# Value products moved into the next pair's first slot in a fused attention and feed-forward kernel, with V casts and part of the K/Q rounding on GpSimd

## The chip, the cores and the metric

The kernel runs on one core of a Trainium2 chip. The metric is the device time of one execution in microseconds. The kernel before took 369.83 us in the median of 14 runs (367.82 to 373.02).

## What is computed

Eight batches of eight heads, 576 positions, head width 64. Attention is limited to a window of 32 positions on each side; eight global positions, drawn at random, see all and are seen by all. Its output is laid out as 4608 rows of 512 and goes through a feed-forward layer with the activation s*relu(h)^2 + b.

```python
scores = scale * np.matmul(q, k.transpose(0, 1, 3, 2))
mask = np.abs(pos[:, None] - pos[None, :]) <= 32
mask = mask | is_global[:, None] | is_global[None, :]
scores = np.where(mask, scores, -1000000000.0)
attn = np.exp(scores - np.max(scores, axis=-1, keepdims=True))
attn = attn / (np.sum(attn, axis=-1, keepdims=True) + 1e-09)
x = np.matmul(attn, v)          # then (batch, position) rows of 8*64
h = np.maximum(x @ w_in, 0.0)   # w_in is 512 x 2048
out = (s * (h * h) + b) @ w_out # w_out is 2048 x 512
```

## The kernel before

**Pairs.** Two heads make a pair, so there are 32 pairs, four to a batch; in the code p is the pair, bi its batch and hp its place in the batch. The keys of a pair lie in five chunks of 120, each with the eight global rows ahead of them (tiles of 128). `qk(p, c)` (line 483) makes the score product pss of chunk c for both heads, ScalarE takes its exponential e (line 487), and VectorE multiplies by the 0/1 mask into em (line 490). `pv(p, parts)` (line 509) makes the value products of all chunks into the PSUM tile po (part 0, weights from vring) and the row sums, against a tile of ones, into its second half (part 1): 14 small matrix products each. There is one po tile. `norm_steps(p)` gives two steps for ScalarE, s1 (Ln of the row sums, line 540) and s2 (Exp of minus that, rep, line 544), and two for VectorE: `sums` (line 527, the parts of the global rows, with a reciprocal and a product at a batch's last pair) and the multiply into xt (line 546), the feed-forward layer's input. When a batch's four pairs are there, `scatter` (line 557) puts its global rows into xt, eight copies on GpSimd, at positions that are held in GpSimd's registers. The `value_load` instructions that fill these registers stand at line 357.

**Feed-forward quanta.** `moe_quanta` works through nine tiles of 512 rows in 32 quanta each: 16 with four products psh (line 580; eight where the tile wraps round in xt), each followed by relu r on ScalarE (line 587) and its square g on VectorE (line 590), then 16 with four products pso each (line 595). A finished row block is stored: the first eight are scaled into held tiles (osbh, line 606) that are completed later by `release` (line 832), since the bias row isn't there yet; the others become osb (line 609). `wpiece` loads w_out again in eight pieces (wst, line 817), and adds on VectorE (wsum, line 821) make from it the bias row, by a product in pair 15 (line 827). psh, pso and others share three PSUM tiles.

**Order by hand.** Each engine works through its instructions in the order in which the program issues them. `run_pair` does pairs 4 to 31 in eight slots: in slots 0 to 4 a score product each, and in each slot nq[s] quanta. What VectorE (and the odd other engine) has to do for a slot's products is put on the list `later` and issued in the next slot, as `prev`. Extra work of a slot (`extra`) is given by the main loop: rounding of natural K and Q to bf16 on ScalarE (`round_nat`, line 182) in slots 5 and 7, the turning of K by a DMA transpose on SP (line 189) in slot 7, that of Q on TensorE (`turn_q`, line 196) in slot 5 with the copies into qbd (line 204) a slot later, weight-sum adds in slots 4 and 7, releases in slot 4. The value products stand in slot 6; Ln and Exp stand in slots 1 and 3 of the following pair. `put_kq` (lines 431 and 435) copies the global columns of K and Q into kt and qbd. Pairs 5 to 7 get K and Q in another way: `trans_a` and `trans_b` turn them on TensorE (line 448) in slot 6 of the pair before, and the copies out of PSUM (kt line 459, qbd line 472, one half on ScalarE and one on VectorE) follow in slot 7.

**V.** The natural rows of V are loaded into natv (line 171; four buffers), cast to bf16 in vring (line 216; four buffers), and the eight global rows are copied in by `put_v` (line 424; by a small DMA on SP, or by VectorE). Up to pair 7 the cast is on ScalarE, from pair 8 on GpSimd, in slot 2 of the pair two before.

**The opening.** `first_pair` does the five score products of pairs 0 to 4 without quanta, with dummy products (line 704) between them. The transposes for the next pair and the value products of the pair before stand in slots 1 and 2 (values in slot 1, row sums in slot 2), Ln at the end of slot 2, Exp in slot 3, the cast of the next pair's V on ScalarE in slot 4, and after it the small DMA of `put_v`. After pair 4's scores come the scatter of batch 0, three memsets on VectorE (lines 810 and 812), and the loop over run_pair, which begins pair 4 at slot 5.

**Loads.** GpSimd's queue issues, in this order: K and Q of pairs 1 to 4 and w_in, the register loads, V of pair 4, K and Q of pair 5, and, between the first pairs, V of pairs 5 and 6, K and Q of pair 6 and two quarters of w_out (line 361). From pair 5 on, SP loads natural K, Q and V four pairs ahead.

The softmax here doesn't subtract the row's maximum and nothing guards it: scores larger than these inputs give would overflow.

## Time and profile before

| what | value |
|---|---|
| median of 14 runs | 369.83 us |
| the profiled execution | 370.58 us |
| its span, first to last instruction | 368.9 us |
| TensorE busy, share of the span | 341.2 us, 92% |
| VectorE busy | 235.3 us, 64% |
| ScalarE busy | 226.1 us, 61% |
| GpSimd busy | 76.5 us, 21% |
| mean granted TensorE clock | 0.975 |
| first feed-forward product starts | 45.39 us |
| last value product starts (pair 31) | about 300.7 us |

"Busy" is the time in which an engine executed an instruction; register loads, branches, semaphores and the issue of hardware DMAs are not in it. A line of a timeline gives the start in us, the duration in us, the engine, the source line, the operation with the tiles out<-in, how many are merged, and in brackets how long the engine had been idle before it and what ended that. PE is TensorE, PEld its weight loads, DVE VectorE, ACT ScalarE, POOL GpSimd, SP SyncE, and a q after a name is that engine's own queue.

### The profile page before, as it was taken

The numbers are of one execution on the slowest core, as the hardware profiler recorded it, in microseconds if no ns is written. First come the engines' busy times: TensorE is split into PE (matmuls) and PEld (weight loads), VectorE is DVE, ScalarE is ACT, GpSimd is POOL, SyncE is SP. The second block draws the span as 40 slices with busy tenths as digits, with TensorE's granted clock in tenths as the row PEclk, the third lists the DMA queues.
The fourth block names the chain that finished last, engine by engine and source line by source line (L and its number), as shares of the span: only waits on it lengthen the run. The fifth ranks groups of instructions, "written<-read, shape, count | busy, mean of one in ns | idle before, by whom it ended". The sixth has DMA issues, their size and how long they took to land.

```text
span 368.9 us, 7680 instructions
## 1 busy us (share of the span) xinstructions
PE 341.2 (92%) x2707; PEld 182.9 (50%) x2743; DVE 235.3 (64%) x634; ACT 226.1 (61%) x440; POOL 76.5 (21%) x160
## 2 busy tenths in 40 slices
PE   5887688889999999999999999999999999999995
PEld 1444443445455545557755455555557644444442
DVE  6755766667887788567766785677666753523521
ACT  5576688845874588458855885589559742602600
POOL 6864293113123400033003000300020001000000
PEclk9578999999999999999999999999999999999999
DMA  7999699999999965587679767775821002002002
GB/s 126 195 210 212 111 164 228 182 207 196 164 168 223 208 129 107 137 198 163 153 176 201 181 147 178 177 148 122 145 80 50 2 34 81 1 37 78 2 38 76
DMA packets 125687, 50.12 MB, mean 136 GB/s; under 512 B 113368, under 2 KB 118488, under 8 KB 125648
## 3 DMA queue, kind: packets, MB, share of 16 engines
q1 hardware_dynamic: 116896, 37.31, 49.8%
q0 software_dynamic: 8544, 12.03, 16.5%
q8 instruction: 21, 0.34, 0.4%
q10 hardware_dynamic: 208, 0.29, 0.3%
q14 instruction: 18, 0.15, 0.1%
HBM read 42.26 MB, written 9.44 MB: 140 GB/s over the span
## 4 chain that ended last, share of the span: by engine, by line
PE 53%; DVE 11%; ACT 10%; issue 9%; DMA 8%; POOL 4%; SPq 2%; POOLq 1%; ACTq 0%; DVEq 0%
PE pso L595 25%; PE psh L580 20%; PE po L509 5%; DMA natv<-in_v_dram 5%; ACT r L587 4%; ACT rep L544 3%; PE pss L483 3%; ACT e L487 2%; DMA gf<-in_q_dram,grow 2%; DVE g L590 2%; DVE xt L546 2%; DVE em L490 2%; SPq L171 1%; DVE osbh L832 1%; DVE wsum L821 1%
## 5 line engine op out<-in xcount | busy, mean ns | idle before, releaser
L580 PE MATMUL psh<-xt,win_t 128*128 128x512 bf16 (+4 forms) x690 | 139.0, 340 | 1.9 <-POOL xt L557 1.0
L595 PE MATMUL pso<-wout_t,g 128*128 128x512 bf16 x559 | 135.6, 379 | 2.3 <-issue 2.1
L587 ACT ACTIVATE r<-psh 128x512 bf16<-128x512 f32 x144 | 90.2, 628 | 54.2 <-PE psh L580 54.0
L487 ACT ACTIVATE e<-pss 128x384 bf16<-128x384 f32 (+1 forms) x160 | 76.8, 485 | 61.7 <-PE pss L483 60.0
L580 PEld LDWEIGHTS <-win_t 128*128 128x128 bf16 x704 | 64.1, 98 | 54.4 <-issue 1.0
L590 DVE TENSOR_TENSOR g<-r 128x512 bf16<-128x512 bf16 x144 | 61.3, 427 | 37.0 <-ACT r L587 35.1
L595 PEld LDWEIGHTS <-g 128*128 128x128 bf16 x576 | 54.8, 98 | 59.7 <-issue 0.6
L490 DVE TENSOR_TENSOR em<-e,mask 128x384 bf16<-128x384 bf16 (+1 forms) x160 | 55.4, 347 | 15.8 <-ACT e L487 14.9
L483 PE MATMUL pss<-qbd,kt 128*128 128x384 bf16 (+1 forms) x160 | 51.5, 326 | 5.0 <-ACT e L487 2.3
L609 DVE SCALAR_TENSOR_TENSOR osb<-pso,s_bc,bias_row 128x512 f32<-128x512 f32 x28 | 20.9, 747 | 40.8 <-PE pso L595 38.1
L557 POOL COPY xt<-xg 128x4 bf16 x64 | 15.2, 238 | 115.3 <-DVE xt L546 111.6
L216 POOL CAST vring<-natv 128x640 bf16<-128x640 f32 x24 | 17.2, 728 | 71.8 <-PE po L509 44.8
L546 DVE TENSOR_TENSOR xt<-po,rep 128x600 bf16<-128x600 f32 x32 | 25.0, 782 | 8.0 <-ACT rep L544 7.8
L509 PE MATMUL po<-em,vring 128*64 128x160 bf16 (+3 forms) x448 | 23.3, 229 | 6.0 <-DVE em L490 3.5
L509 PEld LDWEIGHTS <-vring 128*64 128x64 bf16 x448 | 17.9, 113 | 18.1 <-issue 11.4
L483 PEld LDWEIGHTS <-kt 128*128 128x128 bf16 x160 | 15.7, 100 | 19.9 <-DVE qbd L435 5.2
L544 ACT ACTIVATE rep<-ln 128x640 f32<-128x640 f32 x32 | 24.3, 760 | 0.0
L540 ACT ACTIVATE ln<-po 128x640 f32<-128x640 f32 x32 | 22.7, 709 | 2.6 <-PE po L509 2.3
L204 DVE COPY qbd<-pst 64x600 bf16<-64x600 bf16 x48 | 22.2, 463 | 0.3
L509 PE MATMUL po<-em,onesb 128*64 128x160 bf16 (+2 forms) x448 | 19.8, 223 | 0.0
L182 ACT CAST natbk<-natk 120x640 bf16<-120x640 f32 x24 | 18.4, 767 | 0.0
L182 ACT CAST natbq<-natq 120x640 bf16<-120x640 f32 x24 | 17.4, 725 | 0.0
(104 smaller groups left out, 210.1 us busy)
## 6 DMA issues: line engine op xcount, KB each, us to landing
natv<-in_v_dram SPq DMA_DIRECT2D x55, 150.0 KB
out_dram<-osb SPq DMA_DIRECT2D x28, 256.0 KB
natk<-in_k_dram SPq DMA_DIRECT2D x47, 150.0 KB
natq<-in_q_dram SPq DMA_DIRECT2D x47, 150.0 KB
wst<-in_moe_w_out_dram POOLq DMA_DIRECT2D x8, 512.0 KB, 5.1
win_t<-in_moe_w_in_dram POOLq DMA_DIRECT2D x2, 1024.0 KB, 12.0
wout_t<-in_moe_w_out_dram POOLq DMA_DIRECT2D x4, 512.0 KB, 8.7
out_dram<-osbh SPq DMA_DIRECT2D x8, 256.0 KB
```

What stands on the lines that cost most here:

```text
L182: nc.scalar.copy(out=natb[t][0:KC, p % 2].rearrange("p (c h d) -> p c h d", c=NCH, h=2), in_=nat[t][0:KC, p % NV],)
L483: nc.tensor.matmul(ps[:], ktile[p][:, P * c : P * c + P], qbufs[p % 3][:, :, LO[c] : HI[c]])
L487: nc.scalar.activation(e[:], ps[:], AF.Exp, scale=SCALE)
L490: later.append(lambda: nc.vector.tensor_mul(em[:], e[:], masks[c]))
L509: nc.tensor.matmul(po[D * hh : D * hh + D, a : a + n], onesb[:] if part else vring[:, p % NV, c, hh], emt[(p, c)][:, hh, x : x + n], start ...
L540: nc.scalar.activation(ln[:], po[:, LQ : 2 * LQ], AF.Ln)
L544: nc.scalar.activation(rep[:], ln[:], AF.Exp, scale=-1.0)
L546: lambda: nc.vector.tensor_tensor(out=view(xt[:, hp, x0:], [KC, NCH], [HB, 2], [1, HB]), in0=halves(po[:, 0:LQ]), in1=halves(rep[:]), op=O ...
L580: nc.tensor.matmul(psh[:, d0 : d0 + n], win_t[:, a, f * P : f * P + P], xt[:, a, x0 : x0 + n], start=(a == 0 and j == 0), stop=(a == 3), s ...
L587: nc.scalar.activation(r[:], psh[:], AF.Relu)
L590: later.append(lambda g=g, r=r: nc.vector.tensor_mul(g[:], r[:], r[:]))
L595: nc.tensor.matmul(pso[:], gl[f][:, u * P : u * P + P], wout_t[:, f], start=(f == 0), stop=(f == 15),)
```

## The change

The value products and row sums of pair p move from slot 6 of pair p to slot 0 of pair p+1, behind its first score product; those of pair 31 are issued after the loop. Ln and Exp follow in slots 1 and 2 (they were in slots 1 and 3), and the global sums are issued with the multiply into xt. In the opening the row sums stand in slot 1 and the value products in slot 2, with Ln at the end of slot 1.

The V rows of pairs 1 to 3 are cast on GpSimd right after the issue of w_in, and their small put_v DMAs are issued together before pair 1. Pair 4's cast stays on ScalarE, and its global rows are put by VectorE in pair 4. The register loads move behind the second quarter of w_out. The clearing of natv's first eight rows moves to the front of ScalarE's work, and the memsets of natb and onesf move into pair 5.

For pairs 5 to 7, Q is turned in slot 5 and K in slot 6, and put_kq follows K's copy. The rounding of K and Q for pair p+2 goes to GpSimd where p is over 8 and hp is 1 or 2. The scatter's issue moves from slot 6 to slot 5, and batch 1 gets other counts of quanta in slots 4 and 7, with the same sum.

```diff
-    def round_nat(t, p):
-        nc.scalar.copy(
+    def round_nat(eng, t, p):
+        eng(
...
     nc.vector.memset(qbufs[0][D:P, 0], 0.0)
+    clear(natv[0:NG].rearrange("p n c h d -> p (n c h d)"), NV * NCH * 2 * D)
     nc.scalar.copy(out=six["q"][:NP6, 0].rearrange("p h j d -> p (h j d)"), in_=six0["q"])
...
-    greg_p = [
-        nc.gpsimd.value_load(g32[:1, i, 0:1], min_val=0, max_val=S - 1) for i in range(NG)
-    ]
+    for p in (1, 2, 3):
+        cast_v(nc.gpsimd.tensor_copy, p)
...
         ktile[p] = kt[:]
-        later.append(
-            lambda: nc.vector.tensor_copy(
+
+        def evac():
+            nc.vector.tensor_copy(
                 out=view(kt[:, NG:], [P, NCH], [NJ, KC // NJ], [1, NJ]),
                 in_=view(ps[:], [KC // NJ, NCH], [1, KC // NJ], [NP6, NJ]),
             )
-        )
+            if p >= 5:
+                put_kq(p)
+
+        later.append(evac)
...
-            if p > 1:
+            if 1 < p < 5:
                 put_kq(p)
...
         def s1():
             nc.scalar.activation(ln[:], po[:, LQ : 2 * LQ], AF.Ln)
-            later.append(sums)
 
         def s2():
             nc.scalar.activation(rep[:], ln[:], AF.Exp, scale=-1.0)
+            later.append(sums)
             later.append(
...
             if s < NCH:
                 qk(p, s)
-                if s in (1, 3):
+                if s in (1, 2):
                     step()
+                if s == 4 and hp == 0 and bi > 1:
+                    later.append(lambda: scatter(bi - 1))
...
             elif s == 5:
-                if hp == 0 and bi > 1:
-                    later.append(lambda: scatter(bi - 1))
                 if p == 4:
                     cast_v(A, 5)
-            elif s == 6:
                 if p + 1 < NSIX:
-                    trans_a(p + 1)
                     trans_b(p + 1)
-                pv(p)
-                pending.extend(norm_steps(p))
+            elif s == 6 and p + 1 < NSIX:
+                trans_a(p + 1)
             for f in prev:
                 f()
+            if s == 0:
+                pv(p - 1)
+                pending.extend(norm_steps(p - 1))
...
                 if p:
-                    pv(p - 1, (s - 1,))
-                    if s == 2:
+
+                    pv(p - 1, (2 - s,))
+                    if s == 1:
                         pending.extend(norm_steps(p - 1))
             elif s == 3:
                 step()
-            elif s == 4 and p < 4:
-                cast_v(A, p + 1)
-                if p:
-                    put_v(None, p + 1)
+            elif s == 4 and p == 3:
+                cast_v(A, 4)
...
-            if s == 2:
+            if s == 1:
                 step()
+            if s == 0 and p == 4:
+                put_v(V, 4)
...
-    clear(natv[0:NG].rearrange("p n c h d -> p (n c h d)"), NV * NCH * 2 * D)
...
     put_v(V, 0)
-    put_v(None, 1)
+    for p in (1, 2, 3):
+        put_v(None, p)
...
         elif p == 3:
             load_w_out(1)
+            greg_p = [
+                nc.gpsimd.value_load(g32[:1, i, 0:1], min_val=0, max_val=S - 1)
+                for i in range(NG)
+            ]
...
-    for t in natb.values():
-        nc.vector.memset(t[96:P], 0.0)
...
-    nc.vector.memset(onesf[:], 1.0)
...
-            nq = [0, 1, 1, 1, 0, 1, 1, 2] if hp else [0, 0, 0, 0, 0, 0, 1, 2]
+            nq = [0, 1, 1, 1, 1, 1, 1, 1] if hp else [0, 0, 0, 0, 0, 0, 1, 2]
...
+        if p == 5:
+            for t in natb.values():
+                at(3, nc.vector.memset, t[96:P], 0.0)
+            at(4, nc.vector.memset, onesf[:], 1.0)
         if p >= 6 and p + 2 < NPAIR:
-            at(5, round_nat, "k", p + 2)
-            at(7, round_nat, "q", p + 2)
+
+            eng = G if p > 8 and hp in (1, 2) else A
+            at(5, round_nat, eng, "k", p + 2)
+            at(7, round_nat, eng, "q", p + 2)
...
     flush()
+    pv(NPAIR - 1)
+    pending.extend(norm_steps(NPAIR - 1))
     while pending:
```

## The prediction

> **What bounds the kernel now.** I read the busy table first, then the forty slices, the chain of waits, the timeline around one value product, and the timeline of the opening.
>
> ```profile
> PE 341.2 (92%) x2707; PEld 182.9 (50%) x2743; DVE 235.3 (64%) x634; ACT 226.1 (61%) x440; POOL 76.5 (21%) x160
> ...
> PE   5887688889999999999999999999999999999995
> PEclk9578999999999999999999999999999999999999
> ```
>
> TensorE is the bound, with two weak places: the first 75 us (slices 1 to 8), and a shortage too small for tenths after them. The second is seen in the starts of the first score product of each pair, in TensorE's timeline: pair 8 at 78.71, pair 24 at 230.32, pair 31 at 293.66. Pairs 24 to 30 take (293.66-230.32)/7 = 9.05 us each, pairs 8 to 23 take 151.61/16 = 9.48 us, with the same eight quanta of the feed-forward part. The timeline of pair 21 says why:
>
> ```profile
> 208.11 0.68 DVE L832 TENSOR_TENSOR osbh<-osbh,bias_row 128x512 f32<-128x512 f32 x1
> ...
> 208.16 0.51 PE L509 MATMUL po<-em,vring 128*64 128x160 bf16 x10
> ...
> 208.72 0.32 DVE L490 TENSOR_TENSOR em<-e,mask 128x320 bf16<-128x320 bf16 x1
> ...
> 209.09 0.28 PE L509 MATMUL po<-em,vring 128*64 128x32 bf16 x4 [0.42 <-DVE em L490]
> ```
>
> Ten value products run, then TensorE waits 0.42 us for the last masked tile, which stood on VectorE behind a bias add. Pairs 8 to 15 have a weight-sum add (0.68) in that place, pairs 16 to 23 this release, pairs 24 and later nothing, and there the wait is gone.
>
> The opening has one large hole:
>
> ```profile
> 30.59 0.73 ACT L216 CAST vring<-natv 128x640 bf16<-128x640 f32 x1
> 30.76 0.32 PE L483 MATMUL pss<-qbd,kt 128*128 128x384 bf16 x1 [0.44 <-ACT e L487]
> ...
> 32.96 1.01 PE L509 MATMUL po<-em,vring 128*64 128x160 bf16 x14 [1.50 <-DMA vring<-gvx]
> ```
>
> The V cast of the next pair stands last on ScalarE in each pair (30.59). The small copy of the global rows follows it on SP and takes about 6.5 us to land: that of pair 2 went out at 26.42 and its value product began at 32.96. Pair 3 lasted 37.44-29.81 = 7.63 us, pair 2 lasted 4.93.
>
> **Part 1: the opening, up to the first feed-forward product (45.39).** The copies for pairs 1 to 3 can now go out soon after 18.9, as casts on GpSimd (0.72 each, row L216) follow its weight issue, which ends at 17.2. The natv loads were issued by 12.2 and the first landed at 11.4, so I expect casts until about 20.7, copies landed by 27.5, needed after that. The hole of pair 3 goes: 7.63-4.93 = 2.7. ScalarE has no idle time in pair 2 but 0.37, so a cast less (0.61 from start to start) is worth 0.6 a pair, in pairs 1 to 3: 1.7, as pair 1 hides a little. The row sums ahead let Ln (0.70) start a slot early, but the global sums now run behind the reciprocal of the row sums: 0.23+0.35+0.19 in front of the last xt multiply, so this nets to nothing. Against it: the casts meet VectorE at 17.2 to 19, where the rounding of gb feeds TensorE's global rows; a wait of 0 to 1.4 (none, or two casts), taken as one cast, 0.7. The moved clear (2.32) fits in ScalarE's 2.64 us wait for natq, and bought nothing at 7.29, where the next cast waited for its load anyway. Sum 2.7+1.7-0.7 = 3.7 us.
>
> GpSimd has its own date, though. Its register loads (L357 in the chain of waits) come every 0.59 us, 8 of them 4.7 us, and they now stand between the second W_out load (ends 36.02) and the scatter, which waited there until 43.27:
>
> ```profile
> 35.24 0.78 POOL wout_t L361
> 36.02 7.23 issue
> ```
>
> 36.02+4.7 = 40.7, so the scatter is 2.6 us earlier if GpSimd's loads do not move, 3.7 if they do by a microsecond; nothing shows what held them from 27.24 to 31.24. I take **2.9**, between 1.5 and 5.
>
> **Part 2: pairs 4 to 7.** Pair 4's kt copy no longer stands behind 1.35 us of memsets and behind quanta, so the first score product of pair 5 loses its 0.62 wait: **+0.6**. The memsets in pair 5 lie in VectorE's idle time (1.66 before qbd). In pairs 5 and 6 I count a loss. These rows show the old order:
>
> ```profile
> 56.71 0.60 ACT L587 ACTIVATE r<-psh 128x512 bf16<-128x512 f32 x1 [1.91 <-PE psh L580]
> 57.34 0.65 ACT L472 COPY qbd<-pst 64x600 bf16<-64x600 bf16 x1
> ...
> 58.02 0.77 DVE L472 COPY qbd<-pst 64x600 bf16<-64x600 bf16 x1 [1.66 <-ACT qbd L472]
> ...
> 59.02 0.47 PE L483 MATMUL pss<-qbd,kt 128*128 128x320 bf16 x2 [0.62 <-DVE qbd L435]
> ```
>
> Q's transposes come first now, so behind ScalarE's copy VectorE has qbd 0.70, g 0.4, the V row copy 0.42, kt 0.73, K/Q rows 0.25 = 2.5 us before the next pair can start; it had 1.0. And the value product in slot 0 (1.3 us, from 235.68+0.85 to 237.83) leaves ScalarE without scores. Counted from a pair's start: second exp at 1.8, then Ln, three r, two exps, Exp, cast, two exps and two r more by start-to-start gaps, so ScalarE's copy of Q is at 7.7 to 8.35, next pair at 10.9, against 10.26 (59.02-48.76). Pair 6 has a K rounding (0.5) more in front: 11.4 against 10.42. Loss **1.6**, bounds -3 (one more r and one more wait) and +1.5 (both old TensorE waits of 0.84 and 0.62 gone and none new). Pair 7, with seven quanta and no r, took 9.27 with a wait of 0.93 for em in it; I take most of it: **+0.75**.
>
> **Part 3: pairs 8 to 31.** 16 x (9.48-9.05) = 6.8, less the bias product of pair 15 (0.87), which stays: 6.0 to be had. Nothing is late next on TensorE: its output bank is freed in slot 3 and needed five slots later, the last masked tile has three slots, the vring copies one pair's slot more. ScalarE's fullest windows show 8.20 us a pair with the rounding (1.49) in them, so 6.7 are left. What is late next is VectorE, through GpSimd. 11 pairs (9, 10, 13, 14, ... 29) get two casts more, 22 in all:
>
> ```profile
> 99.48 1.13 DVE L590 TENSOR_TENSOR g<-r 128x512 bf16<-128x512 bf16 x1 [0.15 <-ACT r L587]
> 99.59 0.72 POOL L216 CAST vring<-natv 128x640 bf16<-128x640 f32 x1
> ```
>
> That g took 1.13 instead of 0.42, the length of the cast more. An em at 109.08 took 1.07 beside the cast at 109.19. None of the other casts has such a row; most fall on copies out of PSUM. So a cast costs VectorE 0 to 0.72. The fullest pair, 95.2 to 104.8, has VectorE busy for 8.39 with one such meeting; two more make 9.8, 0.8 above 9.05. At full price that is 4 x 0.8 (pairs 9, 10, 13, 14) and little in the others, about 4 us; the three r buffers hide a part. I take 1.0: **+5.0**, bounds +2 and +7.
>
> [...]
>
> **Part 4: the tail.** After pair 31's products, ten quanta covered the normalising, from 300.83 to the end of the scatter at 307.05; the next tile began at 309.31. Now eight quanta cover it, 8 x 0.86 = 6.9 against 6.2: 0, with 0.6 us left. If that cover is gone, each microsecond more in the chain costs one.
>
> **The sum.** 2.9+0.6-1.6+0.75+5.0 = 7.65. The profiled execution took 370.58 (span 368.9 and 1.7 around it): 362.9. It lies 0.75 above the median 369.83, so the median becomes **362.2**.
>
> **The rivals.**
> 1. *The gain is given back on VectorE* (or the waits for em were not the cause): pairs 8 to 23 stay near 9.4 and only the opening's 2 to 3 us remain: 367. For it: VectorE at 8.39 of 9.6. Against: pairs 24 to 30 show 9.05 with the same products.
> 2. *Everything the waits held comes free*: opening 4.5, pairs 4 to 7 at +2, pairs 8 to 23 at 6.5: 13 us, 357. For it: ScalarE loses both the casts and the rounding. Against: the register loads' date.
> 3. *The value product in slot 0 starves ScalarE* (slower). For 1.3 us no score product is made; ScalarE then has Ln and Exp (1.46) in slots 1 and 2, and the two score buffers make TensorE wait the same 1.3. It decides where ScalarE's busy time is over 9.05-1.3 = 7.7 us a pair. The windows show 4.6, 6.5, 8.2, 6.6 in a batch: only the third is over, and it is relieved of 1.49. If all 27 pairs paid half of it, that is 17.5, less 7.65, on 369.83: 379.7.
> 4. *The moved copies change nothing early*: V loads land late, the hole of pair 3 stays, and pairs 5 and 6 lose 3: the whole near 369.
>
> **How the numbers follow.** Forecast (359 to 366.5) 0.62; rival 2 0.12; rival 1 0.13; rival 4, within 0.3% 0.05; rival 3 and worse 0.08. A measurement can tell 0.3%, 1.1 us, from no change. So faster 0.87, same 0.05, slower 0.08. The range joins the low ends of the bounds (1.5+0.6-3+0.75+2 = 1.9) with the gains of rival 2 (13): 356.5 to 367.5.
>
> **What would show it.** Right: no wait of a value product for em after pair 7; first score products about 9.05 to 9.15 apart from pair 8 on; no wait for vring's copy near 30; first feed-forward product near 42.5, right after a row of register loads. Pairs 5 and 6 as long as before or longer, with VectorE's kt copy last in front of the score product. Wrong: g or em rows of 1.1 in each of pairs 9, 10, 13, 14 with pairs over 9.3; ScalarE's exp as what score products wait for in slots 2 to 4; V casts on GpSimd waiting for their loads past 22; the scatter of the last batch behind the last quantum.

## The result, and the profile after

The changed kernel takes **375.09 us** (median of 10 runs, 372.95 to 375.59). The kernel before it took 370.47 us (median of all its 47 runs by then, 367.82 to 373.02). The ratio is 1.0114, 95% interval 1.0088 to 1.0140: slower by about 1.1%, where the prediction said 2% faster (362.2 us, range 356.5 to 367.5). The profiled execution took 375.79 us with a span of 374.1 us, against 370.58 and 368.9 before.

The page of the changed kernel, in the lines that the prediction showed of the one before:

```profile
PE 345.3 (92%) x2707; PEld 181.5 (49%) x2743; DVE 243.5 (65%) x635; ACT 215.3 (58%) x415; POOL 96.1 (26%) x185
...
PE   5778598799999989999999999999999999999995
PEclk9569989989999999999999999999999999999999
```

ScalarE has lost 11 us of work and GpSimd has gained 20, as the change meant. VectorE has one instruction more and 8 us more busy time: something makes its instructions longer. TensorE, with the same 2707 products, is busy 4 us longer: some of them ran at a lower granted clock (mean 0.968, 0.975 before). In the last row the 8s in slices 6 and 9 (of 9.35 us each, so about 47 to 56 and 75 to 84 us) are places of such a clock; before, the row is at 9 from slice 5 on.

The start of each pair's first score product, in TensorE's timeline, says where the time went:

| stretch | before, us | changed, us | change | predicted |
|---|---|---|---|---|
| to the first score product of pair 1 | 19.00 | 21.59 | +2.6 | |
| to that of pair 4 | 37.44 | 37.19 | -0.25 | |
| to the first feed-forward product | 45.39 | 45.70 | +0.3 | -2.9 |
| from there to pair 8 | 33.32 | 36.39 | +3.1 | +0.25 |
| pair 8 to pair 31 | 214.95 | 216.10 | +1.15 | -5.0 |
| pair 31 to the end | 75.24 | 75.91 | +0.7 | 0 |

From the first feed-forward product to the end of the loop the changed kernel has one pair's value products (1.05 us) still to do that the old one had done. Read with that, the third row is +1.35 and the last -0.4; the two between them are not touched, since the products are outstanding at both of their ends.

The waits of TensorE in the changed kernel, over the whole span (what waits, for what; us in total, times, longest):

```profile
PE pss L487 <- DVE qbd L435: 8.0, 12, 1.8
PE psv L410 <- DVE em L494: 3.5, 1, 3.5
PE psh L584 <- POOL xt L561: 2.6, 1, 2.6
```

No value product waits for a masked tile any more; before, that was the first row of this view:

```profile
PE po L509 <- DVE em L490: 3.5, 8, 0.9
```

In its place stand 8.0 us in which a pair's first score product waits for `put_kq`, the end of the K/Q placing on VectorE, which was 1.8 us before; a wait of 3.5 us in the opening (0.92 before); and 2.6 us in front of the scatter (0.99 before). TensorE's own view already tells that three new waits took the place of the old one. The rows behind each:

**The opening**, in the timeline of pair 0:

```profile
16.36 3.07 DVE L341 SCALAR_TENSOR_TENSOR mask<-band,notg,gadd 128x192 bf16<-128x192 f32 x2
17.10 2.16 POOL L216 CAST vring<-natv 128x640 bf16<-128x640 f32 x3
20.24 1.02 PE L410 MATMUL psv<-gb,ident 128*8 128x64 bf16 x16 [3.50 <-DVE em L494]
```

The same two rows before:

```profile
16.37 0.70 DVE L340 SCALAR_TENSOR_TENSOR mask<-band,notg,gadd 128x192 bf16<-128x192 f32 x2
17.66 1.01 PE L410 MATMUL psv<-gb,ident 128*8 128x64 bf16 x16 [0.92 <-DVE gb L403]
```

Two mask instructions that took 0.70 us together before take 3.07 beside the three GpSimd casts. Everything behind them on VectorE is 2.4 us later, the rounding of `gb` among it, and the products that wait for it start at 20.24 instead of 17.66.

**The scatter of pair 4**, in windows (us; busy time and instructions of TensorE, its weight loads, VectorE, ScalarE, GpSimd; granted clock; DMA share; GB/s):

```profile
41.00:45.70 4.70, 1.38 (x27) 0.90 (x26) 3.95 (x12) 2.71 (x5) 1.66 (x8) 1.00 0.26 44
45.70:50.00 4.30, 4.24 (x12) 1.60 (x12) 1.11 (x6) 1.19 (x2) 4.21 (x6) 0.60 0.63 88
```

Before, pair 4's value products stood there and the first feed-forward products ran like this:

```profile
43.35 0.61 PE L509 MATMUL po<-em,vring 128*64 128x160 bf16 x14 [0.16 <-DVE xt L546]
45.39 2.75 PE L580 MATMUL psh<-xt,win_t 128*128 128x512 bf16 x11 [0.99 <-POOL xt L557]
```

Without those value products TensorE has 1.38 us of work in 4.7 us there, and in the next window the mean granted clock is 0.60 (0.5 from 46.3 to 49.7 us). The first feed-forward products, which took 2.75 us before, take 4.44. The same happens behind a wait of 1.84 us in front of pair 7: a clock of 0.5 from 73.6 to 77.1 us, and pair 7 takes 9.85 us.

**Pair 17**, one of the pairs with first feed-forward products and with rounding on GpSimd:

```profile
174.42 0.91 POOL L182 CAST natbq<-natq 120x640 bf16<-120x640 f32 x1 [4.26 <-ACT r L591]
174.67 1.20 DVE L839 TENSOR_TENSOR osbh<-osbh,bias_row 128x512 f32<-128x512 f32 x1
...
177.42 0.18 DVE L435 COPY qbd<-gqd 128x80 bf16<-128x80 bf16 x1
...
177.66 0.30 PE L487 MATMUL pss<-qbd,kt 128*128 128x320 bf16 x1 [0.74 <-DVE qbd L435]
```

The release takes 1.20 us instead of 0.68 beside the cast; the placing, which stands behind it on VectorE and ends with this `qbd`, ends late; and the first score product of pair 18 waits 0.74 us for them. Such pairs take 9.5 to 10.4 us up to pair 22. The pairs with second products are at 9.01 to 9.02, a little below the predicted 9.05 to 9.15; only pair 15, with the bias product (9.87), and pairs 16 and 20 (9.29 and 9.28) are longer.

### The profile page after: what moved, and what is told of

Same layout as the page of the kernel before. It is cut to its first block, busy times and chain, and to the rows that moved or that the text cites. A ratio compares the mean times of both kernels' runs of the same rounds, so it can differ in the third digit from the quotient of the medians.

```text
span 374.1 us, 7664 instructions
## 1 busy us (share of the span) xinstructions
PE 345.3 (92%) x2707; PEld 181.5 (49%) x2743; DVE 243.5 (65%) x635; ACT 215.3 (58%) x415; POOL 96.1 (26%) x185
## 4 chain that ended last, share of the span: by engine, by line
PE 64%; DVE 19%; ACT 6%; issue 6%; POOLq 1%; DMA 1%; POOL 1%; ACTq 0%; DVEq 0%
PE pso L599 30%; PE psh L584 18%; PE po L513 7%; PE pss L487 5%; DVE g L594 4%; DVE em L494 3%; DVE qbd L204 2%; DVE xt L550 2%; ACT r L591 2%; ACT e L491 2%; ACT ln L544 1%; DMA natk<-in_k_dram 1%; POOLq L805 1%; PE pst L196 1%; DVE kt L431 1%
## 5 line engine op out<-in xcount | busy, mean ns | idle before, releaser
L591 ACT ACTIVATE r<-psh 128x512 bf16<-128x512 f32 x144 | 88.8, 616 | 59.7 <-PE psh L584 57.8
L594 DVE TENSOR_TENSOR g<-r 128x512 bf16<-128x512 bf16 x144 | 63.1, 447 | 41.6 <-ACT r L591 41.5
L494 DVE TENSOR_TENSOR em<-e,mask 128x384 bf16<-128x384 bf16 (+1 forms) x160 | 60.6, 382 | 34.1 <-ACT e L491 33.8
L216 POOL CAST vring<-natv 128x640 bf16<-128x640 f32 x27 | 21.0, 792 | 54.8 <-PE po L513 44.7
L513 PE MATMUL po<-em,vring 128*64 128x160 bf16 (+3 forms) x448 | 19.8, 225 | 0.4 <-ACT ln L544 0.4
L513 PEld LDWEIGHTS <-vring 128*64 128x64 bf16 x448 | 15.8, 111 | 8.3 <-issue 6.5
L513 PEld LDWEIGHTS <-onesb 128*64 128x64 bf16 x448 | 15.0, 113 | 1.3 <-DVE xt L550 1.1
L709 PE MATMUL psw<-dummy 128*128 128x512 bf16 x32 | 14.0, 504 | 1.7 <-DVE dummy L228 1.3
```

The lines of the kernel that those rows point to most:

```text
L494: later.append(lambda: nc.vector.tensor_mul(em[:], e[:], masks[c]))
L513: nc.tensor.matmul(po[D * hh : D * hh + D, a : a + n], onesb[:] if part else vring[:, p % NV, c, hh], emt[(p, c)][:, hh, x : x + n], start ...
L591: nc.scalar.activation(r[:], psh[:], AF.Relu)
L594: later.append(lambda g=g, r=r: nc.vector.tensor_mul(g[:], r[:], r[:]))
```

## The experiments

The theory: VectorE is late in three places (casts on GpSimd in pair 0; the chain ahead of pairs 6 and 7; the placing in the pairs with first products, which the value products in slot 6 had covered for 1.3 us), and TensorE's new idle time in pairs 4 and 6 costs a second time through the granted clock. The rivals: the rounding on GpSimd is the whole loss of pairs 8 to 31; ScalarE is starved by the value products in slot 0; the opening or the queues set pairs 4 to 7. Times are medians; each ratio is to the kernel before on the same chip, with its 95% interval. The median of the kernel before lay between 369.3 and 372.7 from one set of runs to another, so kernels of different sets are compared by ratios and by the stretches of their profiles.

| run | on which kernel | time, us | ratio |
|---|---|---|---|
| e1 V casts back on ScalarE | changed | 373.22 | 1.0076 (1.0047-1.0105) |
| e2 rounding back on ScalarE | changed | 372.47 | 1.0087 (1.0057-1.0117) |
| e3 Q transposes a slot earlier | changed | 380.28 | 1.0278 (1.0246-1.0309) |
| e4 pair 4's value products back | changed | 373.99 | 1.0096 (1.0061-1.0131) |
| e5 additions and releases in slots 1, 2 | changed | 374.41 | 1.0064 (1.0028-1.0101) |
| e6 move undone from pair 7 | changed | 378.43 | 1.0180 (1.0097-1.0264) |
| e7 pairs 4 to 7 in the old order | changed | 374.77 | 1.0096 (1.0064-1.0129) |
| e8 four edits of these | changed | 369.58 | 0.9956 (0.9917-0.9994) |
| e9 memsets earlier | changed | 375.78 | 1.0103 (1.0041-1.0164) |
| e10 six mends | changed | 367.32 | 0.9858 (0.9788-0.9928) |
| e11 e10, one place copy on ScalarE | e10 | 375.26 | 1.0069 (1.0041-1.0098) |
| e12 e10, pairs 5 to 7 in the changed order | e10 | 367.27 | 0.9888 (0.9824-0.9951) |
| e13 one gap filled | changed | 372.72 | 1.0083 (1.0042-1.0123) |
| e14 e10, one gap filled | e10 | 365.15 | 0.9864 (0.9795-0.9933) |
| e15 row sums first alone | before | 371.19 | 1.0025 (0.9988-1.0062) |
| e16 the move alone from pair 8 | before | 368.28 | 0.9956 (0.9918-0.9993) |
| e17 three gaps filled | changed | 372.53 | 1.0064 (1.0032-1.0097) |
| e18 e12, one gap filled | e12 | 367.08 | 0.9896 (0.9856-0.9935) |

### The opening: e1 and e15

e1:
```
-    for p in (1, 2, 3):
-        cast_v(nc.gpsimd.tensor_copy, p)
...
-            elif s == 4 and p == 3:
-                cast_v(A, 4)
+            elif s == 4 and p < 4:
+                cast_v(A, p + 1)
+                if p:
+                    put_v(None, p + 1)
...
-    for p in (1, 2, 3):
-        put_v(None, p)
+    put_v(None, 1)
...
-            if s == 0 and p == 4:
-                put_v(V, 4)
```

> The changed kernel with the V casts of pairs 1 to 3 back on ScalarE, one in slot 4 of the pair ahead, and each pair's V rows placed there as before; value products, rounding split and the rest stay. Theory (the three GpSimd casts in a row hold up VectorE in pair 0, and that delays pair 1): the first score product of pair 1 comes back from 21.59 us to 19.0, and pairs 2 to 4 run as in the changed kernel, so that the time falls by 1 to 2.6 us, to 372.5-374. Rival (the casts off ScalarE are what closed the hole of pair 3): pair 3 takes 7.6 us again, and the 2.6 us won in pair 0 are given back, time 374.5-376.

The masks in the timeline of e1's pair 0:

```profile
16.36 0.70 DVE L341 SCALAR_TENSOR_TENSOR mask<-band,notg,gadd 128x192 bf16<-128x192 f32 x2
```

The masks are back at 0.70 us and pair 1 starts at 19.00; pair 3 still takes 4.87 us. The 2.6 us stay won up to the end (pair 31 starts 2.7 us earlier, the span is 371.8). So the three casts in a row cost 2.6 us in this profile, and they are not what closed the hole of pair 3. (In the profiles of e5, e6 and e7, whose pair 0 begins 1 to 2 us later, the same casts cost about 1.5 us: pair 0 takes 8.45 to 8.56 us, against 6.95 without the casts.) For that, e15 has only the order of sums and values of the change, on the kernel before:

```
-                    pv(p - 1, (s - 1,))
-                    if s == 2:
+                    pv(p - 1, (2 - s,))
+                    if s == 1:
...
-            if s == 2:
+            if s == 1:
                 step()
```
(with the guards of `pv` that go with it, and `sums` queued by the exponential's step, as in the change).

> The kernel before, with one part of the change alone: in pairs 1 to 4 the row sums of the pair before come ahead of its value products, and the logarithm goes from slot 2 to slot 1; casts, register loads and all the rest as before. Theory (this part alone closed the 2.7 us hole of pair 3): pair 3 goes from 7.6 to 4.9 us and the time falls by 2 to 3 us, to 367.5-369. Rival (the register loads behind pair 3, or the casts, closed it): pair 3 stays at 7.6 us, time 370-371.

Pair 3 takes 4.88 us: the order alone closes the hole, as the theory had it, and pair 4 starts at 33.93 instead of 37.44. The time did not fall, though. Pair 4 took 13.38 us for 11.32: its value products waited 1.38 us for the DMA of the global V rows, which now comes too late for pair 4 (in the full change VectorE places them), and the granted clock behind that wait was 0.5 (from 41.5 to 44.9 us). And pairs 8, 12, 16 and 20 took 9.66 us for 9.26, because the global sums, which feed the scatter of those pairs, are made a step later; that is 1.7 us from pair 8 to 31, a cost of the change that nobody had counted.

### The rounding and the move: e2, e6, e16

e2:
```
-            eng = G if p > 8 and hp in (1, 2) else A
+            eng = A
```

> The changed kernel with all K/Q rounding on ScalarE, as before the change. Theory (the loss of pairs 8 to 31 comes from the K/Q placing standing late in VectorE's order, since the value products no longer cover it; GpSimd's share of the rounding only makes it somewhat later): the pairs with feed-forward first products still run at 9.3-9.7 us, time within 1.5 us of the changed kernel's 375. Rival (it is the rounding on GpSimd, which slows VectorE beside it): those pairs come to 9.0-9.1 us, and the time falls by 4 to 6 us, to 369-371.

Pairs 13, 17 and 21, where the rounding met a release or an addition, go from 10.07-10.41 to 9.54-9.57; the other pairs with first products stay at 9.5. Pairs 8 to 31 take 213.75 us for 216.10. Each theory has its part: the rounding on GpSimd costs 2.35 us, and without it the placing is still late.

e6 undoes the move alone, from pair 7 on:
```
+                if p >= 7:
+                    pv(p)
+                    pending.extend(norm_steps(p))
...
-            if s == 0:
+            if s == 0 and p <= 7:
                 pv(p - 1)
```
(with the logarithm and the exponential in slots 1 and 3 from pair 8, and no products behind the loop).

> The changed kernel with the value products back in the pair's own slot 6 from pair 7 on (logarithm and exponential in slots 1 and 3 from pair 8), everything else as changed, the rounding on GpSimd too. Theory (one wait took the place of another: the products in slot 6 wait 0.3 us for the last masked tile but cover 1.3 us of the K/Q placing): pairs of second products go from 9.02 to about 9.26, pairs of first products come to 9.5-9.7 also where GpSimd rounds beside a release (10.07 now), the stretch from pair 8 to pair 31 changes by -2 to +0.5 us, time 373-375.5. Rival (the move was a gain of its own in pairs 8 to 31, and only GpSimd's rounding costs): the stretch gets 3 us longer, time 377-379.

Wrong for the theory: the stretch became 218.47 us, 2.4 more, and the time lies in the rival's range. The pairs with second products went to 9.26, and the four behind a batch's last pair (8, 12, 16, 20) to 9.66, as in e15, where no rounding is on GpSimd: in the old order the later `sums` stand in front of the masked tile. The pairs with first products stayed at 9.5 to 10.4. Alone, on the kernel before, it is e16:

```
-                pv(p)
-                pending.extend(norm_steps(p))
+                if p < 8:
+                    pv(p)
+                    pending.extend(norm_steps(p))
...
+            if s == 0 and p > 8:
+                pv(p - 1)
+                pending.extend(norm_steps(p - 1))
```
(with the steps in slots 1 and 2 from pair 9, and the scatter a slot earlier).

> The kernel before, with one part of the change alone: from pair 8 on the value products run in the next pair's slot 0 (with logarithm and exponential in slots 1 and 2 and the scatter a slot earlier); rounding, casts and pairs 0 to 7 as before. Theory (the wait for the last masked tile, 0.3 us in most pairs, is exchanged for a wait for the K/Q placing in pairs of first products): the pairs of second products go from 9.26 to 9.02, those of first products stay at 9.5, time down by 0.5 to 1.5 us, to 369-370. The prediction's own claim for this part (5 us, with nothing late next): 365-366.

Pairs with second products 9.26 to 9.02, pairs with first products 9.6 to 9.53, as the theory says; pairs 8 to 31 gain 1.8 us (212.14, and 1.05 for the products that stand outside at the end, against 214.95). The time fell by a little more than the theory gave, to a ratio of 0.9956. The waits of TensorE between 78 and 300 us set side by side, in us, each from that view of its kernel:

| kernel | value products for the masked tile | score products for the placing | pairs 8 to 31 |
|---|---|---|---|
| before | 2.5 | none | 214.95 |
| e15, later sums | 4.4 | none | 216.65 |
| e6, later sums, rounding on GpSimd | 5.2 | none | 218.47 |
| e16, move alone | none | 1.4 | 213.19 |
| e2, move, later sums | none | 1.6 | 213.75 |
| changed: move, later sums, rounding on GpSimd | none | 3.8 | 216.10 |

(e16's stretch with the 1.05 added.) One wait is exchanged for another, of half its size where VectorE is as before (2.5 to 1.4), of a third with the later sums (4.4 to 1.6), of three quarters with all of the change (5.2 to 3.8). Read down the last column, the move is worth 1.8 us by itself, the rounding on GpSimd costs 1.8 (e15 to e6) to 2.35 (e2 to changed), and the later sums cost 1.7 in the old order and 0.55 behind the move. So -1.8, +0.55 and +2.35 make the measured +1.15.

### Ways to place earlier: e3, e5, e11

e3:
```
-            at(5, turn_q, p + 1)
+            at(4, turn_q, p + 1)
```

> The changed kernel with the Q transposes of the next pair, and so the K/Q placing behind them on VectorE, one slot earlier (slot 4 for 5); nothing else differs. Theory (in pairs 7 to 31 the first score product waits for the placing): the placing is done about 1.2 us earlier, the waits of the score products for it go, and with 12 to 16 pairs at 9.05-9.1 us for 9.5-9.7 the time falls by 4 to 7 us, to 368-371. Rival (ScalarE is starved when the value products run in slot 0, and the pairs are long for that): no pair gets shorter by more than 0.1 us, the time stays at 374-376.

Neither happened: pairs with first products became 9.98 to 10.05 us (pair 13 10.23). In the timeline of pair 18:

```profile
183.85 0.44 PE L196 MATMUL pst<-ident,natbq 128*128 128x128 bf16 x5 [0.78 <-ACT e L491]
```

The next score product has no wait any more, so the placing is early enough. But the transposes, this row, take one of the two score buffers of PSUM, and in slot 4 they wait 0.78 us until ScalarE has read it: with the logarithm and the exponential among its work, ScalarE runs without a break from 179.87 us to the end of that exponential. Twelve such waits, 9.1 us, replace eight of 3.8 us. The first cure failed, and the rival about ScalarE has a point: its slack in slots 1 to 4 is gone.

e5:
```
-            for s in (4, 7):
+            for s in (1, 2):
                 if adds:
                     at(s, adds.pop(0))
...
-            at(4, release)
+            at(1, release)
```

> The changed kernel with the additions that are not tied to a slot (the weight-row sums of pairs 7 to 14, the releases of held rows of pairs 16 to 23) given to VectorE in slots 1 and 2, where it idles 0.7 to 1.7 us a slot, and no longer in slots 4 and 7. Theory (VectorE is behind from slot 3 to slot 5 of the pairs with first products, so that the K/Q placing ends after TensorE wants it; 0.68 us of addition stands ahead of it there): those pairs of 9.5-10.4 us in the stretch from pair 9 to pair 23 get 0.3 to 0.7 us shorter, ten to twelve of them, and the time falls by 2.5 to 5 us, to 370-372.5. Rival (ScalarE's late relus are what makes VectorE late, the additions fit in its gaps): at most 0.5 us off the whole, 374.5-375.

With the releases in slot 1, pairs 17, 18, 21 and 22 go from 10.09, 9.54, 10.07 and 9.53 to 9.47, 9.19, 9.46 and 9.30: the backlog on VectorE is what the placing waits for, and pairs 16 to 23 together take 2.4 us less. The theory's 2.5 to 5 us were not reached: the sums in slots 1 and 2 cost 0.7 of that in pairs 9 to 15, and the loss is one row of pair 9:

```profile
99.22 0.72 POOL L216 CAST vring<-natv 128x640 bf16<-128x640 f32 x1
99.23 2.31 DVE L594 TENSOR_TENSOR g<-r 128x512 bf16<-128x512 bf16 x1
99.87 0.72 POOL L182 CAST natbk<-natk 120x640 bf16<-120x640 f32 x1
100.54 0.72 POOL L182 CAST natbq<-natq 120x640 bf16<-120x640 f32 x1
```

The three GpSimd casts ran in a row again, and `g` (0.42 alone) took 2.31 us, as long as all three; the first score product of pair 10 then waited 1.84 us for the placing behind it. In the changed kernel the same three hit an `em` of pair 9 (2.54 us), early in the pair, where there was room for it.

e11, on e10:
```
-            for hh in range(2):
+            for hh, eng in ((1, nc.scalar.copy), (0, nc.vector.tensor_copy)):
```

> The kernel with six mends, and of the two Q copies that place a turned pair from pair 8 on, one on ScalarE beside the other on VectorE. Theory (in the pairs of first products TensorE waits 0.2 to 0.4 us for the K/Q placing behind VectorE's backlog; one copy is 0.47 us): pairs of first products from pair 16 on go from 9.19 to 9.02-9.10, some 12 pairs by 0.1 to 0.3 us, time 1 to 3 us below the kernel with six mends. Rival (ScalarE is as late as VectorE in slots 5 and 6, with the rounding there): the wait only changes its name, time within 0.7 us of it or above.

The rival, and dearly: pairs with first products became 10.0 us. The timeline of pair 18:

```profile
169.33 0.81 ACT L182 CAST natbk<-natk 120x640 bf16<-120x640 f32 x1
...
170.66 0.65 ACT L204 COPY qbd<-pst 64x600 bf16<-64x600 bf16 x1
...
172.04 0.31 PE L483 MATMUL pss<-qbd,kt 128*128 128x320 bf16 x1 [0.70 <-DVE qbd L433]
```

ScalarE's copy stands behind the K rounding and a relu, later than VectorE would have done it: a wait of 0.70 us in twelve pairs, 8.0 us in all between 78 and 300 us; in e14, which has VectorE make both copies, that row is 1.1 us in four. In these slots ScalarE has no more room than VectorE.

### Pairs 4 to 7: e4, e7, e9, e13, e17

e4:
```
-            if s == 0:
+            if s == 0 and p > 5:
                 pv(p - 1)
                 pending.extend(norm_steps(p - 1))
+            if s == 6 and p == 4:
+                pv(4)
+                pending.extend(norm_steps(4))
```

> The changed kernel with the value products of pair 4 alone back in pair 4's slot 6, ahead of the first feed-forward products, which wait for the scatter; all later pairs keep the move. Theory (TensorE idles in front of the scatter without them, and the granted clock of the next stretches falls): the clock of 45.7 to 50 us goes from 0.60 towards 1.0, pair 5 loses 1.3 us of work and regains some 1.7 us of clock, pair 5's start comes 0 to 1.3 us earlier; time down by 1.5 to 3 us, to 372-373.5. Rival (the gap and the clock are paid by something else, such as the chain of pair 5 on ScalarE and VectorE): pair 5 starts and ends as in the changed kernel, time within 0.5 us of it.

A part of it. Pair 5 takes 10.32 us for 10.87, but TensorE still stood 1.11 us in front of the scatter, the clock still fell to 0.5 (45.8 to 49.2 us), and the twelve products took 4.44 us. The ratio differs from the changed kernel's by less than its interval.

e13 fills the gap and moves nothing:
```
+            if p == 4 and s == 6:
+                warm(11)
             Q(nq[s])
```

> The changed kernel with eleven products of zeros (2.4 us at the full clock) on TensorE in pair 4 ahead of the feed-forward products that wait for the scatter, and nothing else. Theory (the 2.6 us in which TensorE stands still there cost a second time, because the granted clock is 0.5-0.6 for some 4 us behind it): the first eleven feed-forward products take 2.7 us for 4.4, pair 5 starts 1.5 us earlier, time 373-374. Rival (the clock falls for another reason, or the time is given back behind pair 5's other waits): the clock stays at 0.6 there, or pair 8 starts as late as before; time 374.5-375.5.

The first feed-forward products in the timeline of e13:

```profile
45.26 2.75 PE L584 MATMUL psh<-xt,win_t 128*128 128x512 bf16 x12
```

2.75 us for 4.44, at a clock of 1.0; pair 5 starts at 47.85 for 49.98, and the 2.1 us are still there at pair 31. Of these, 1.7 are the edit's (pair 4 takes 11.10 us for 12.79); the other 0.4 are the opening's, since pair 4 began that much earlier in this profile. So the idle time in front of the scatter cost its second price through the clock, and eleven useless products take it back. The second fall, in pair 7, is unchanged in e13 (0.5 from 71.5 to 74.9 us). e17 adds seven products of zeros at the end of pairs 5 and 6:

```
             Q(nq[s])
+            if p in (5, 6) and s == 7:
+                warm(7)
```

> The changed kernel with the eleven products of zeros in pair 4 and seven more at the end of pair 5 and of pair 6, where TensorE waits 1.55 and 1.84 us for the K/Q placing. Theory (the clock of 0.5-0.75 from 72 to 77 us follows from those waits): with all three gaps filled the clock stays at 1.0 from 45 to 80 us, pair 7 takes 8.2 us for 9.85, and pair 8 starts 1 to 1.7 us earlier than with the first gap filled alone. Rival (the zeros take a PSUM bank and stand ahead of the placed pair, and that costs as much; or the clock falls there for another reason): pair 8 starts within 0.4 us of where it did, or later.

The clock is 1.0 from 45 to 80 us, pair 7 takes 8.16 us for 9.85, and pair 8 starts at 78.94 (80.02 in e13), from pair 4 to pair 8 1.3 us less: the theory, though pair 6 paid 0.4 for the zeros. One reserve belongs here. Whether the clock falls behind a gap varies: with 2.6 us in front of the scatter it fell in all seven profiles that have that gap, with 1.7 us (e12) too, with about 1.1 us (before, e4, e7, e10, e11) in two of five, and never in the four whose gap was filled (e13, e14, e17, e18). Behind the wait of 1.84 us in front of pair 7 it fell in five profiles (changed, e1, e4, e5, e13) and not in five others (e2, e3, e9, e12, e18).

The traces tell most of what decides. Wherever a profile shows stretches at 0.5 up to 300 us, they last 3.41 us or a multiple of it, and they begin and end on one grid of 3.41 us, which lies elsewhere in each profile: in the changed kernel, 46.33 to 49.74 and 73.64 to 77.05 us, the starts 27.31 us or eight steps apart; in e1, 43.4 to 46.8 and 70.7 to 74.1. Four windows of it in the changed kernel (columns as above):

```profile
42.92:46.33 3.41, 0.76 (x11) 0.43 (x7) 3.04 (x10) 0.95 (x2) 2.20 (x9) 1.00 0.02 3
46.33:49.74 3.41, 3.41 (x9) 1.22 (x8) 0.81 (x3) 1.19 (x2) 3.41 (x6) 0.50 0.71 95
70.23:73.64 3.41, 1.57 (x32) 1.07 (x32) 2.61 (x8) 1.23 (x3) 0.00 (x0) 1.00 1.06 157
73.64:77.05 3.41, 3.41 (x10) 1.32 (x9) 0.91 (x4) 2.20 (x4) 0.72 (x1) 0.50 1.03 181
```

Of all such windows at full clock between 30 and 300 us, the clock fell behind each of the 14 in which TensorE, transposes apart, was busy for 1.2 us or less, behind 5 of the 13 with 1.3 to 1.6 us, and behind none of the others. So a gap counts by where it lies on the grid: the same 1.1 us in front of the scatter left 1.15 us of products in one window of e10 and no window of e11 with less than 1.33, and the clock fell in e10 alone.

The price agrees with the length of the stretch: 3.41 us at half rate cost 1.7 us of work, and 4.44 - 2.75 = 1.7 here. The windows behind which the clock fell were not idle: they held up to 1.57 us of products (the third row above). Transposes are left out of the count because the windows sort better without them: between 41.5 and 45.7 us TensorE had nothing but transposes (two groups of 0.45 us), and with transposes counted, the windows with 1.6 to 2.05 us of work stand on both sides. No run here separates transposes from idle time.

e7:
```
-            nq = [0, 1, 1, 1, 1, 1, 1, 1] if hp else [0, 0, 0, 0, 0, 0, 1, 2]
+            nq = [0, 1, 1, 1, 0, 1, 1, 2] if hp else [0, 0, 0, 0, 0, 0, 1, 2]
...
+                    trans_a(p + 1)
+                    trans_b(p + 1)
+                if p < 8:
+                    pv(p)
+                    pending.extend(norm_steps(p))
```
(and the K/Q placing behind Q's copy again, the steps in slots 1 and 3 up to pair 8).

> The changed kernel with pairs 4 to 7 in the old order (value products in the own slot 6, both transposes there, K/Q placing behind the second, quanta as before the change); opening and pairs 8 to 31 as changed. Theory (the new order of pairs 4 to 7 loses about 3.6 us: the idle time at the scatter, a lower granted clock behind it, and the longer chain of pairs 5 and 6): the stretch from pair 4 to pair 8 goes from 44.9 to 41.3-42.5 us, time 371.5-373. Rival (the stretch is longer because of what the opening leaves behind: the register loads, rounding or loads that come later): it stays at 44-45 us, time 374.5-375.5.

Not confirmed: the stretch from pair 4 to pair 8 took 44.38 us, where the kernel before took 41.27 with this order. Pair 5 alone took 12.93 us for 10.26. In e8, which has the same pairs 4 to 7 and shows the same 12.92, VectorE's timeline names what is new in it:

```profile
52.42 0.59 DVE L866 MEMSET natbq<- 32x640 uint32 x1
...
53.47 0.77 DVE L546 TENSOR_TENSOR xt<-po,rep 128x600 bf16<-128x600 f32 x1
...
54.30 0.97 PE L509 MATMUL po<-em,vring 128*64 128x160 bf16 x13 [0.88 <-DVE xt L546]
```

This memset and the one of `natbk` before it (0.59 too), which the change moved into pair 5, stand ahead of the normalization of pair 4, and in the old order pair 5's value products wait for that, in slot 6; the clock fell behind that wait (0.5 from 54.6 to 58.0 us). e9 moves the memsets alone, in the changed kernel:

```
-        if p == 5:
+        if p == 4:
             for t in natb.values():
-                at(3, nc.vector.memset, t[96:P], 0.0)
-            at(4, nc.vector.memset, onesf[:], 1.0)
+                at(6, nc.vector.memset, t[96:P], 0.0)
+            at(6, nc.vector.memset, onesf[:], 1.0)
```

> The changed kernel with the three memsets that it runs on VectorE in slots 3 and 4 of pair 5 (the pad rows of the two rounded K/Q tiles, the ones) put into slot 6 of pair 4, where VectorE idles in front of the scatter. Theory (they are 1.35 us in front of the last masks of pair 5, ahead of everything that pair 6's placing waits for): pair 5 goes from 10.87 to 9.6-10.3 us, time down by 0.5 to 1.5 us, to 373.5-374.6. The prediction's rival (they lie in VectorE's idle time): pair 5 stays at 10.9, time 374.8-375.2.

No gain: pair 5 took 12.16 us, pair 7 8.16 with no fall of the clock, and pair 8 started 44.48 us behind pair 4 for 44.90. Pair 5's 12.16 us are not the edit's: e6, which is the changed kernel up to pair 6, shows the same 12.16, with the same idle time of 1.73 us in front of ScalarE's second exponential in that pair (0.45 in the profile of the changed kernel); what causes it is open. That the memsets do no harm in the changed order, as the prediction said, is seen better with pair 4's value products in their place: pair 5 takes 10.32 us with the memsets in it (e4), and 10.36 and 10.32 without (e12, e18).

### Together: e8, e10, e12, e14, e18

e8 is the edits of e1, e2, e5 and e7 in one kernel.

> Four edits together on the changed kernel: V casts of pairs 1 to 3 on ScalarE, all K/Q rounding on ScalarE, pairs 4 to 7 in the old order, additions and releases in slots 1 and 2. If the four causes are separate, the gains add: 2.3 (measured) + 2.5 (measured) + 2.5 to 3.6 + 2 to 4, time 363 to 366, faster than before the change (370.2). If the loss is one bound that shows in several places (ScalarE's work), they add to half of it: 368-370.

The gains added to less than their sum, and the time lies in the second range, of 368 to 370. The memsets just shown are a reason that needs no common bound; e10 tests it. 0.9956 is still below the kernel before. e10 adds to e8 the memsets of e9 and leaves the weight-row sums and pair 4's V rows as the change has them:

```
-                if p:
+                if 0 < p < 3:
                     put_v(None, p + 1)
...
+            if s == 0 and p == 4:
+                put_v(V, 4)
...
-            for s in (1, 2):
+            for s in (4, 7):
                 if adds:
```

> The changed kernel with: V casts of pairs 1 to 3 on ScalarE, all K/Q rounding on ScalarE, pairs 4 to 7 in the old order, the memsets in slot 6 of pair 4, pair 4's V rows placed by VectorE and not by a DMA, releases (but not the weight-row sums) in slot 1. What is kept of the change: row sums first with earlier logarithm and exponential in the first pairs, value products in the next pair's slot 0 from pair 8, register loads behind pair 3. Theory (the same old order of pairs 4 to 7 took 44.5 us in the run before it because the memsets in pair 5 delayed its normalization, then the value products, and the clock fell behind that gap; the DMA for the V rows of pair 4 added 0.9): pair 5 comes from 12.92 to about 10.3, the stretch from pair 4 to pair 8 to 41.3-42 us, time 364.5-367.5, faster than before the change. Rival (the stretch is long for another reason than the memsets): it stays at 44 us, time 368.5-370.

Pair 5 came to 10.65 us and pairs 16 to 23 to 9.01-9.30, and the time is 367.32, ratio 0.9858. The stretch from pair 4 to pair 8 took 43.8 us, because the clock fell to 0.5 in front of pair 5, from 42.5 to 49.4 us (in e11, the same code up to there, it did not, and the stretch took 42.34). e12 has the changed order in pairs 5 to 7 (Q turned in slot 5, K in slot 6 with the K/Q placing behind its copy, and the changed counts of quanta go with that order):
```
-                if p < 8:
-                    pv(p)
+            if s == 6 and p == 4:
+                pv(4)
```

> The kernel with six mends, but with pairs 5 to 7 in the changed order (value products in the next pair's slot 0, Q transposes in slot 5, K transposes in slot 6) and only pair 4's value products in its own slot 6. Theory (the changed order makes pair 6's and pair 7's placing wait for a chain on ScalarE and VectorE that the value products used to cover): pairs 5 and 6 take 10.3 and 11.4 us against 10.3 and 10.3, the clock falls behind the waits of 1.5 to 1.8 us, and the time is 1.5 to 4 us above the kernel with six mends. Rival (the memsets and the casts were all that was wrong in pairs 4 to 7): within 1 us of it.

367.27 us: level with e10, the rival. Both have a clock of 0.5 in pair 4 (in e12 from 41.4 to 48.2 us), which hides the comparison. e14 and e18 fill the gap of e10 and e12, with `warm(4)` and `warm(7)` in the place of e13's.

> The kernel with six mends, with four products of zeros in pair 4 ahead of the feed-forward products (its gap there is 1.1 us and the clock behind it was 0.5 for 5 us). Theory: those twelve products take 2.75 us for 5.28, pair 5 starts 2 us earlier, time 364.5-366.5. Rival (the clock falls by chance, in some executions and not in others, or the zeros themselves lead to it): within 1 us of 367.3.

> The kernel with six mends in which pairs 5 to 7 keep the changed order (365.4 us span, clock 0.5 for 6 us behind a gap of 1.7 us in pair 4), with seven products of zeros in that gap. Theory (with the clock out of the way, the changed order of pairs 5 to 7 costs what its longer chain costs, 10.4 + 11.4 against 10.3 + 10.3-11.1 for the old order, and no more): the first feed-forward products take 2.75 us for 5.28, the span falls by 2 to 2.5 us, to 363-363.5, and the time to 364.5-365.5, level with the old order when filled (365.15). Rival (the changed order's waits of 1.5 to 1.8 us ahead of pairs 6 and 7 let the clock fall later instead): the gain is given back there, time 366.5-367.5.

In both the first feed-forward products took 2.75 us for 5.28. **e14 has the lowest time and the shortest span of the study**, 365.15 and 363.9 us, 0.9864 of the kernel before (0.9795 to 0.9933); by that ratio it cannot be told from e10 (0.9858). e18 came to 367.08, in its rival's range. Its profiled execution, the slowest of its six, doesn't show the rival's reason: the clock stays at 1.0 behind the waits in front of pairs 6 and 7. It lost 4.1 us later (pairs 8 to 31 take 215.98 us, 211.88 in e12): at 97.23 us the first score product of pair 10 waited 2.77 us for the placing, which had waited 2.55 us for the K transpose by DMA (`kt<-natbk`), and the clock was 0.5 behind it, from 97.3 to 100.7 us. e8 had such a wait of VectorE, of 2.6 us up to 79.8, e14 none. What the other five executions of e18 lost is not known. Up to pair 8 the two orders are within 0.3 us (pair 4 to pair 8: 42.8 with the outstanding products counted, against 43.1). So the changed order of pairs 5 to 7, with its cover put back in pair 4 and its gap filled, costs nothing that these two profiles can tell up to pair 8.

## Why the prediction was wrong

Point by point, by its own steps.

**Part 1, the opening (predicted -2.9, measured +0.3, or +1.35 with the outstanding products).** Right: the hole of pair 3 goes, by 2.8 us (a part of it was the clock, which the prediction did not see: 0.5 from 32.8 to 36.2 us in the profile of before, from the end of the wait of 1.50 us on), and the register loads end when they were said to (41.4 us in the chain of waits, forecast 40.7). They are not what the scatter waits for: it stands until 43.56 for the last `xt` of pair 3, and that has the opening's delay in it; in e1, without the delay, the first feed-forward product starts at 43.13. Wrong in its cause and in its costs. The prediction put the closing down to the early casts; e15 shows that the order of sums and values does it, with the casts where they were. A cast less on ScalarE was to give 0.6 us a pair; pair 2 went from 4.93 to 4.87. And the step that failed most is "a wait of 0 to 1.4 (none, or two casts), taken as one cast, 0.7": it measured 2.6. All three casts held VectorE up, and in the profiled execution not at the rounding of `gb` but at the masks ahead of it, which the prediction did not list.

**Part 2, pairs 4 to 7 (predicted +0.25, measured +3.1).** The chain of pairs 5 and 6 is right to the tenth in the profiled execution: 10.87 and 11.39 us, forecast 10.9 and 11.4, with `kt` and `put_kq` last ahead of the score product. So close a hit is in part luck: e5 and e6 have the same program up to there, and pair 5 takes 11.64 and 12.16 us in their profiles. The memsets are harmless in that order, as it said (e4 beside e12 and e18). The wait for pair 5's placing is gone, as it said. What it left out is the work that moved away: pair 4's value products stood in front of the scatter, and without them TensorE idles 2.6 us, and the clock falls to 0.5 for 3.4 us. It checked where each wait would go, and not where new idle time would come. From pair 4 to pair 8, e13 puts 1.6 us on this clock and e17 another 1.3 on that of the second gap; together that is 2.9 of the 3.1, and what is left is near the forecast's 0.25.

**Part 3, pairs 8 to 31 (predicted -5.0, measured +1.15).** Right: no value product waits for `em`, the pairs with second products are at 9.01-9.02, and the cost named as late next was VectorE through GpSimd. The step that failed is "Nothing is late next on TensorE". It looked at the output bank, the masked tile and V rows, and not at the next pair's own operands: the placing starts behind the transposes in slot 5, and the value products in slot 6 had given it 1.3 us. A second size was off in the same step: "6.0 to be had" came from the lengths of pairs, 9.48 against 9.05, but in that stretch the view of waits has only 2.5 us for the masked tile. The rest was VectorE's backlog, which releases and sums make and which holds up whatever waits for VectorE next (releases in slot 1 shorten pairs 16 to 23 by 2.4 us in e5); the move shifts that wait and removes only a part of it. e16 measures the move at -1.8 for the -6.0, e2 the rounding at 2.35 for the 1.0 that was taken, and the later sums, which the prediction had counted at nothing, at 0.55.

**Part 4, the tail** held: the outstanding products apart, it is 0.4 us shorter.

**The rivals.** The result is on the side of rival 3, but not by its mechanism: no score product waits for ScalarE in pairs 8 to 31 of the changed kernel. ScalarE's loss of slack is real and shows only when something else is asked of slots 4 to 6 (e3, e11). Rival 1, the gain given back on VectorE, is what happened in pairs 8 to 31; it kept the opening's gain, and so ended at 367.

**The price of a cast.** "So a cast costs VectorE 0 to 0.72" was read off rows of before with one cast each (there was one more: a copy of the global columns of K took 0.73 us, 0.17 alone, beside the cast at 256.21). Three casts in a row held a VectorE instruction for 2.3 to 2.5 us (a `g` for 2.31 in pair 9 of e5, an `em` for 2.54 in pair 9 of the changed kernel), 1.9 and 2.2 more than they take alone (0.42 and 0.32): near the upper end for each of the three, and all of it on one instruction. The sum was far from paid in full, though: 22 casts at 0.72 would be 15.8 us of VectorE time; VectorE is busy for 243.5 us in the changed kernel and 239.7 in e2, and 2.35 us of that reached the time.

**The range.** Its ends are a little low by the prediction's own terms: 369.83 less 1.9 and less 13 are 367.9 and 356.8, for the 367.5 and 356.5 that it gives. The result lies more than 7 us above the upper one either way.

Not settled: what decides behind a window with 1.3 to 1.6 us of products, what holds ScalarE in pair 5 of e6 and e9, and why the K transpose was late in e8 and e18 and not in e14.

## What to carry to other kernels

Before work is moved away from a place, list what it covers there: here 1.3 us of value products hid a placing on VectorE, and 1 us of them kept TensorE busy in front of a scatter. A wait on a backlogged engine is removed by taking work off that engine's queue ahead of it (releases into idle slots: 2.4 us in eight pairs); moving the waiting instruction only exchanged it for another (e3, e11). A gain read off the length of a stage should be checked against the sum of the waits that the profile names in it.

## What the runs showed that was not expected

- GpSimd casts of 0.72 us that follow one another at once can hold a VectorE instruction for as long as all of them take: 2.31 us for a `g` of 0.42, 3.07 for two masks of 0.35. Not always: in the opening of e5 VectorE got in between, the two masks took 1.71 us and the casts 2.43 for 2.16.
- A TensorE gap of 2.6 us between transposes and the next products was followed in seven of seven profiles by a granted clock of 0.5, which stretched 2.75 us of products to 4.3-5.3; eleven products of zeros in the gap removed it.
- The clock falls and comes back on a grid of 3.41 us that lies elsewhere in each execution, and it fell behind windows of it with up to 1.57 us of products.
- The same program up to pair 6 (e10 and e11) took 13.56 and 11.87 us for pair 4, by the clock alone: single profiles of this opening differ by 1.7 us without any edit.
